# Three transposes for two per 128 slots, and both scatters of a one-unit block behind its second pair of ReLUs

## The chip, the cores and the metric

The kernel runs on one core of one Trainium2 chip. The metric is the device time of one execution in microseconds (us). Before the change three runs took 1338.32, 1340.45 and 1340.85 us; the median is 1340.45 us.

## The reference

A convolution over 7 tokens is followed by a mixture of experts. `x` has 8 sequences of 3584 tokens with 192 channels. Each of 8 heads (24 channels) has 7 taps, made from `weight` by a softmax. The result of the convolution goes to 8 experts: each token uses one, the one with the largest gate logit, or the expert of the token before it where a local gate is at 0.5 or above.

```python
x = einsum('hk,bskhg->bshg', softmax(weight), windows(x))      # 8 x 3584 x 192
logits = x @ w_gate                                            # 192 x 8
local  = sigmoid(x @ w_local)
for b, s:
    e = argmax(logits[b, s]) if s == 0 or local[b, s] < 0.5 else e_before
    out[b, s] = softmax(logits[b, s])[e] * (relu(x[b, s] @ w1[e]) @ w2[e])   # 192 -> 1024 -> 192
```

All arithmetic is in 32-bit floats.

## The kernel before

**Tiles and stages.** The 28,672 tokens are cut into 16 parts of 1792. For each part the kernel computes the convolution (VectorE, line 388, with a first tap on ScalarE, line 378), the gate logits and the route, and then scatters every token's row from SBUF to its slot in a DRAM tensor `slots`, in which the slots of one expert lie together. A row (`DG` = 259 floats) holds a scale, a token number, the 192 channels from column `Y0` on, 64 channels once more (columns `Y0 + D` to `IX`), and the token number as an integer. A scatter is an indirect DMA of GpSimd (line 777, issued by `put`), 128 rows at a time.

**Blocks.** The expert layers run over blocks of slots. A unit is 128 slots of one expert; a block has one unit (n = 1) or two (n = 2). The trace has 142 blocks: first 35 of one unit, which run while the first parts are still being made, then 87 of two units, then 20 of one unit. A block needs its expert's weights (one tile `wb`, 1536 KB, line 906, loaded three blocks ahead into one of four buffers) and its rows (`xg`, line 913).

**One block in TensorE's order.** `hidden` multiplies the rows, channels on partitions (`xT`), by `w1` (line 963) in two halves of 24 matmul instructions in the trace each; after each half ScalarE writes two ReLUs into `hT` (line 968). Below they are called the first and the second pair of ReLUs. Then `turn` makes `xT` of the next block: it transposes `xg` on TensorE (line 360) into PSUM, `xps`, and ScalarE copies it to SBUF (lines 947 and 949). Then `output` multiplies `hT` by `w2` (line 980): the first half of its matmuls reads what the first pair of ReLUs wrote, the second half needs the second pair. ScalarE scales one half of the result (line 988), VectorE adds the other (line 992), and GpSimd scatters it to the output (line 996). All these orders are written out by hand; every engine runs its list in that order. `step` puts convolution and routing work in between, by times written in the code.

**Halves.** Each matmul works on 64 partitions, and two such matmuls, one for each half of the partitions, run beside each other. Of the 192 channels each half therefore sees three groups of 64 (`KD` = 3, index d), in an order that the host writes into `w1` (`_w1_layout`). `turn` before the change transposes two pieces of 128 columns per unit, each for both halves of the slots (`turn_half`): four transposes per unit. These give both halves of the partitions two of their three groups; the third one lies in PSUM on the other half of the partitions, and ScalarE copies it across (line 949, one copy for each half).

**Scatters of slots between ReLUs.** `hidden` calls `put(relu)` after each pair of ReLUs, for every block but the first: the scatter is made to wait for that ReLU. `shares=(1, 1)` says how many scatters go behind each pair. Nothing is issued when no rows are waiting. In blocks of two units a third may go behind the copy of `turn`.

Of the kernel before, what the change touches and what calls it, by code (L numbers as in the profile page):

```python
# [17 lines left out]
P = 128  # L18
# [63 lines left out]
def kernel(  # L82
# [112 lines left out]
    def wide(g, xv, y_sb, both):  # L195

        lps = yps_p.tile([P, 512], F32, name="yps")[:, :4 * TB].rearrange("p (q s) -> p q s", s=TB)  # L200
        count = [0]

        def mine():
            count[0] += 1
            return both and count[0] % 2 == 0

        def convolve(half, heads):
            bs = slice(half * NH, (half + 1) * NH)
            for h in heads:
                ps = hps_p.tile([P, 512], F32, name="hps")[:TB, :NH * GS]  # L210
                nc.tensor.matmul(ps, lhsT=hank[:NI, h, :],
                                 rhs=xv[:NI, bs, h * GS:(h + 1) * GS], start=True, stop=True)
                to = y_sb[:TB, bs, Y0 + h * GS:Y0 + (h + 1) * GS]
                at = ps.rearrange("p (b d) -> p b d", d=GS)
                if mine():
                    nc.vector.tensor_scalar(to, at, rz[:TB, h:h + 1], None, Alu.mult)
                else:
                    nc.scalar.activation(to, at, Act.Copy, scale=rz[:TB, h:h + 1])
                yield

        def again(half):
            bs = slice(half * NH, (half + 1) * NH)
            nc.gpsimd.tensor_copy(yr[:, bs, :], y_sb[:TB, bs, Y0 + P:Y0 + D])
            nc.gpsimd.tensor_copy(y_sb[:TB, bs, Y0 + D:IX], y_sb[:TB, bs, Y0 + P:Y0 + D])

        def turned(half, qs):
            at = half * 3 * NH // 2
            for q in qs:
                tps = hps_p.tile([P, 512], F32, name="hps")[:, :4 * TB].rearrange(
                    "p (u s) -> p u s", s=TB)  # L230
                for u in range(4):
                    b = half * NH + (q * 4 + u if q < 2 else 2 * u)
                    src = (y_sb[:TB, b, Y0:Y0 + P] if q < 2
                           else yr[:, b:b + 2, :].rearrange("p b d -> p (b d)"))
                    nc.tensor.transpose(tps[:, u, :], src, identity=ident[:TB, :TB])
                leave = nc.vector.tensor_copy if mine() else nc.scalar.copy
                leave(yT[:, at + 4 * q:at + 4 * q + 4, :], tps)
                yield

        def products():  # L240
            for j in range(4):
                u = j // 2 * 3 * NH // 2 + j % 2 * 4
                nc.tensor.matmul(lps[Q * j:Q * j + Q], lhsT=wgb[:, 0, :], rhs=yT[:, u:u + 4, :],
                                 start=True, stop=False, skip_group_check=True)
            for i in range(2):
                for j in range(4):
                    u = j // 2 * 3 * NH // 2 + NH + j % 2 * 2
                    nc.tensor.matmul(lps[Q * j:Q * j + Q, i::2, :], lhsT=wgb[:, 1 + i, :],
                                     rhs=yT[:, u:u + 2, :], start=False, stop=(i == 1),
                                     skip_group_check=True)  # L250

        yield from convolve(0, range(H))
        zy = z_tile()
        yT = zy[:, :3 * NH * TB].rearrange("p (u s) -> p u s", s=TB)
        yr = zy[:TB, 3 * NH * TB:].rearrange("p (b d) -> p b d", d=DR)
        again(0)
        yield from convolve(1, range(5))
        yield from turned(0, (0, 1))
        yield from convolve(1, range(5, H))
        yield from turned(0, (2,))  # L260
        again(1)
        yield from turned(1, range(3))
        products()
        if both:
            nc.vector.tensor_copy(lsb[:, :2, :], lps[:, :2, :])
            nc.scalar.copy(lsb[:, 2:, :], lps[:, 2:, :])
        else:
            nc.scalar.copy(lsb, lps)
        yield
        ltp = yps_p.tile([P, 512], F32, name="yps")[:TB].rearrange("p (q c) -> p q c", c=P)  # L270
        for q in range(4):
            nc.tensor.transpose(ltp[:, q, :], lsb[:, q, :], identity=ident)
        lt = sm.tile([P, NB, E + 1], F32, name="lt")[:TB]
        mark["lt", g] = nc.vector.tensor_copy(lt.rearrange("p (j q) e -> p j q e", q=4),
                              ltp.rearrange("p q (j c) -> p j q c", c=Q)[:, :, :, :E + 1])
        got[g] = lt
# [77 lines left out]
    def halves():  # L354
        return [(half, slice(half * DR, (half + 1) * DR)) for half in range(2)]
# [203 lines left out]
    def gathered(ps):  # L559
        xg = xp.tile([P, KT, DG], F32, name="xg")  # L560
        nc.scalar.copy(xg[:, 0, :Y0 + D], ps[:, :Y0 + D])
        nc.scalar.copy(xg[:, 0, Y0 + D:IX], ps[:, Y0 + P:Y0 + D])
        nc.scalar.copy(xg.bitcast(I32)[:, 0, IX:], ps[:, 1:2])
        return xg

    def logits(g, y_sb):

        nc.gpsimd.tensor_copy(y_sb[:, :, Y0 + D:IX], y_sb[:, :, Y0 + P:Y0 + D])  # L568
        z = z_tile()[:, :NT * D].rearrange("p (t d) -> p t d", d=D)
        for t in range(0, NT, TQ):  # L570
            u = min(t + TQ, NT)
            nc.vector.transpose(z[:, t:u, :], y_sb[:, t:u, Y0:Y0 + D])  # L572
            yield 0.2 * (u - t)
        yield "hop"


        lps = [hps_p.tile([P, TQ * Q], F32, name="hps") for half in range(2)]
        begin = [min(TQ * j, NT - TQ) for j in range(4)]
        for b in range(DQ):
            for j in range(4):  # L580
                for half, rows in halves():
                    nc.tensor.matmul(lps[half][Q * j:Q * j + Q, :], lhsT=wgq[rows, b, :],  # L582
                                     rhs=z[rows, begin[j]:begin[j] + TQ, b * Q:(b + 1) * Q],
                                     start=(b == 0), stop=(b == DQ - 1))
        ls = sm.tile([P, 2, TQ * Q], F32, name="ls", bufs=1)
        for half in range(2):
            nc.scalar.copy(ls[:, half, :], lps[half])
        yield "hop"
        lq = sm.tile([P, 2 * TQ, Q], F32, name="lq", bufs=1)
        nc.vector.transpose(lq.rearrange("p t e -> p (t e)"), ls.rearrange("p h x -> p (h x)"))  # L590
        yield 0.4
        lt = sm.tile([P, NT + 2, E + 1], F32, name="lt")
        for r in range(4):
            for j in range(4):
                t, u = TQ * j, min(TQ * (j + 1), NT)
                at = r // 2 * TQ + t - begin[j]
                e0 = r % 2 * (E + 1)
                nc.vector.tensor_copy(lt[Q * r:Q * r + Q, t:u, :],  # L598
                                      lq[Q * j:Q * j + Q, at:at + u - t, e0:e0 + E + 1])
                yield 0.12  # L600
        return lt
# [328 lines left out]
    def turn(n, xg):  # L930


        xps = xps_p.tile([P, 2, 512], F32, name="xps")
        at = xps[:, :, :BT].rearrange("p h (d k s) -> p h d k s", d=2, k=KT)
        for d in range(2):
            for k in range(n):
                src = xg[:, k, Y0 + d * P:Y0 + (d + 1) * P]
                for half in range(2):
                    turn_half(at[:, half, d, k, :], src, half)
        xT = tp.tile([P, KD, BT], F32, name="xT")  # L940
        to = xT.rearrange("p d (k h s) -> p h d k s", k=KT, h=2)
        first, by = to[:, :, :2], at
        if n == KT:
            first, by = [a.rearrange("p h d k s -> p h (d k) s") for a in (first, by)]
        else:
            first, by, to, at = [a[:, :, :, 0, :] for a in (first, by, to, at)]
        nc.scalar.copy(first, by)  # L947
        for half, rows in halves():
            copied = nc.scalar.copy(to[rows, :, 2], at[(DR, 0)[half]:(P, DR)[half], :, 0])  # L949
        return xT, copied  # L950

    def hidden(n, wb, xT, shares=(1, 1)):
# [4 lines left out]
        for two in range(2):  # L957
# [8 lines left out]
            for half in range(2):  # L966
                m = half * 4 + two * 2
                relu = nc.scalar.activation(hT[:, m:m + 2, w], hps[half][:, :, w], Act.Relu)  # L968
            for _ in range(shares[two]):
                put(relu)  # L970
        return hT

# [195 lines left out]
def _w1_layout(np, w1):  # L1168


    w = w1.reshape(E, KD, DR, 2, F // 2).transpose(0, 3, 2, 1, 4)
    w = np.stack([w[:, 0][:, :, [0, 2, 1]], w[:, 1][:, :, [1, 2, 0]]], 1)
    return w.reshape(E, P, KD * F // 2)


# [57 lines left out]
```

## Time and profile before

| what | value |
|---|---|
| median of three runs | 1340.45 us |
| the profiled execution's own time | 1340.85 us |
| its span, first to last instruction | 1339.1 us |
| TensorE busy (line 360: transposes) | 1315.2 us (60.3 us) |
| ScalarE busy (lines 947 and 949: copies of `turn`) | 583.9 us (72.2 and 92.4 us) |
| GpSimd busy (line 777: scatters to `slots`) | 492.8 us (228.0 us) |
| VectorE busy | 778.6 us |

The profiled execution's own time is 0.4 us above the median, and 1.75 us of it lie outside the span. Busy time of TensorE is the union of its matmuls, whose ends are modelled, so 98% busy is not 98% of its peak; the distance from the start of one block to that of the next tells more. A row of the timeline gives start, length, engine, line, operation, tiles, shapes and count, and in brackets how long the engine was idle before it and what ended that. One matmul in the code is two in the trace; one transpose is one.

### The profile page before, as it was taken

What the parts mean: (1) busy time and instruction counts of PE and PEld (TensorE: products, weight loads), DVE (VectorE), ACT (ScalarE), POOL (GpSimd) and SP (SyncE); (2) the same over time, 40 slices, a digit from 0 to 9 for tenths busy, and PEclk for the clock granted to TensorE, in tenths of its full rate; (3) what the DMA queues carried; (4) which work ended last, traced back from release to release, by engine and by line L of the source; (5) the groups of instructions that cost most, each with busy time, mean ns of one, the idle gap of its engine ahead of it and who ended that gap; (6) DMA issues with size and microseconds to landing.
All of it is one profiled execution on the core that took longest, in us unless ns stands there. A gap on an engine that the chain in (4) does not pass through costs nothing. (4 is left out here: it accounts for less than half of the span.)

```text
span 1339.1 us, 41274 instructions
## 1 busy us (share of the span) xinstructions
PE 1315.2 (98%) x16682; PEld 1264.3 (94%) x16682; DVE 778.6 (58%) x2434; ACT 583.9 (44%) x1431; POOL 492.8 (37%) x538
## 2 busy tenths in 40 slices
PE   8899999999999999999999999999999999999997
PEld 7898999899999999999999999999999999999997
DVE  5878887877777777868786878786520000000000
ACT  5244544444444444444444444444334333334443
POOL 4455443534343434343434343434344211121111
PEclk9899999999999999999999999999999999999999
DMA  4799999977575857675767675756566655556893
GB/s 180 262 357 406 376 352 356 365 281 276 192 287 189 295 197 286 209 274 208 274 209 274 208 281 207 288 204 234 206 234 230 207 185 184 190 192 235 322 332 124
DMA packets 67298, 340.36 MB, mean 254 GB/s; under 512 B 12576, under 2 KB 23191, under 8 KB 47650
## 3 DMA queue, kind: packets, MB, share of 16 engines
q1 hardware_dynamic: 44784, 284.88, 59.2%
q0 software_dynamic: 22320, 52.82, 10.4%
q8 instruction: 133, 2.18, 0.6%
q14 instruction: 59, 0.48, 0.1%
q10 hardware_dynamic: 2, 0.00, 0.0%
HBM read 284.73 MB, written 53.41 MB: 253 GB/s over the span
## 5 line engine op out<-in xcount | busy, mean ns | idle before, releaser
L980 PE MATMUL yps<-wb,hT 64*128 64x192 f32 x7328 | 647.0, 326 | 8.2 <-ACT hT L968 5.3
L963 PE MATMUL hps<-xT,wb 64*128 64x256 f32 (+1 forms) x6816 | 634.5, 336 | 1.6 <-issue 1.2
L980 PEld LDWEIGHTS yps<-wb,hT 64*128 64x128 f32 x7328 | 603.7, 187 | 19.6 <-ACT hT L968 10.8
L963 PEld LDWEIGHTS hps<-xT,wb 64*128 64x128 f32 x6816 | 585.1, 187 | 28.7 <-issue 3.2
L996 POOL DMA_INDIRECT out_dram<-o_sb,xg x229 | 232.4, 1015 | 608.6 <-DVE o_sb L992 540.1
L968 ACT ACTIVATE hT<-hps 128x512 f32<-128x512 f32 (+1 forms) x568 | 262.1, 512 | 393.1 <-PE hps L963 271.6
L388 DVE SCALAR_TENSOR_TENSOR y_sb<-x_sb,c,y_sb 128x336 f32<-128x336 f32 x672 | 376.1, 569 | 20.1 <-ACT y_sb L378 2.0
L992 DVE SCALAR_TENSOR_TENSOR o_sb<-yps,xg,o_sb 128x192 f32<-128x192 f32 x229 | 87.5, 413 | 475.7 <-ACT o_sb L988 468.5
L777 POOL DMA_INDIRECT slots<-y_sb,posi x228 | 228.0, 1000 | 207.4 <-ACT hT L968 81.6
L988 ACT ACTIVATE o_sb<-yps,xg 128x192 f32<-128x192 f32 x229 | 86.9, 418 | 305.4 <-PE yps L980 299.7
L949 ACT COPY xT<-xps 64x256 f32<-64x256 f32 (+1 forms) x284 | 92.4, 325 | 7.0
L947 ACT COPY xT<-xps 128x512 f32<-128x512 f32 (+1 forms) x142 | 72.2, 509 | 5.9 <-PE xps L360 2.9
L360 PEld LDWEIGHTS xps<-ident,xg 64*128 64x128 f32 x916 | 60.2, 139 | 5.2
L378 ACT ACTIVATE y_sb<-x_sb,c 128x336 f32<-128x336 f32 x112 | 63.7, 581 | 1.0
L360 PE MATMUL xps<-ident,xg 64*128 64x64 f32 x916 | 60.3, 221 | 0.0
L572 DVE STREAM_TRANSPOSE z<-y_sb 128x768 f32<-128x768 f32 (+1 forms) x56 | 45.4, 852 | 0.4
L598 DVE COPY lt<-lq 32x36 f32<-32x36 f32 x224 | 41.0, 183 | 3.5
L582 PE MATMUL hps<-z,wg 64*32 64x128 f32 x1344 | 24.1, 272 | 0.7 <-issue 0.5
L582 PEld LDWEIGHTS hps<-z,wg 64*32 64x32 f32 x1344 | 19.0, 105 | 3.1 <-issue 2.3
L556 PE MATMUL yps<-y_sb 112*128 112x194 f32 x64 | 13.8, 377 | 1.8 <-DVE y_sb L550 1.8
L556 PEld LDWEIGHTS yps<-y_sb 112*128 112x128 f32 x64 | 12.5, 220 | 2.6 <-DVE y_sb L550 2.0
L568 POOL COPY y_sb<-y_sb 128x896 f32<-128x896 f32 x14 | 13.4, 954 | 0.0
(240 smaller groups left out, 384.0 us busy)
## 6 DMA issues: line engine op xcount, KB each, us to landing
wb<-in_w_dram SPq DMA_DIRECT2D x138, 1536.0 KB
x_sb<-in_x_dram SPq DMA_DIRECT2D x14, 1920.0 KB
xg<-slots SPq DMA_DIRECT2D x87, 259.0 KB
xg<-slots SPq DMA_DIRECT2D x53, 129.5 KB
wb<-in_w_dram SPq DMA_DIRECT2D x12, 512.0 KB
out_dram<-o_sb,xg POOLq DMA_INDIRECT x229
slots<-y_sb,posi POOLq DMA_INDIRECT x228
x_sb<-in_xb_dram SPq DMA_DIRECT2D x4, 768.0 KB
```

The costliest lines, as they stand in the source:

```text
L360: nc.tensor.transpose(to, src[rows], identity=ident[rows, rows])
L378: nc.scalar.activation(cols(h), chans(h, 0), Act.Copy, scale=c[:, h, 0:1])
L388: nc.vector.scalar_tensor_tensor(cols(h), chans(h, k), c[:, h, k:k + 1], cols(h), Alu.mult, Alu.add)
L777: ins = nc.gpsimd.indirect_dma_start(out=slots[:, :], in_=rows, in_offset=None, out_offset=bass.IndirectOffsetOnAxis(ap=to, axis=0)).ins
L947: nc.scalar.copy(first, by)
L949: copied = nc.scalar.copy(to[rows, :, 2], at[(DR, 0)[half]:(P, DR)[half], :, 0])
L963: nc.tensor.matmul(hps[half][:, j, w], lhsT=wb[rows, f0:f0 + P], rhs=xT[rows, d, w], start=(d == 0 and j == 0), stop=(d == KD - 1), skip_g ...
L968: relu = nc.scalar.activation(hT[:, m:m + 2, w], hps[half][:, :, w], Act.Relu)
L980: nc.tensor.matmul(yps[half][:, k * D:(k + 1) * D], lhsT=hT[rows, m, k * P:(k + 1) * P], rhs=wb[rows, WA + m * D:WA + (m + 1) * D], start= ...
L988: nc.scalar.activation(o_sb[:, k, :], y[k][0], Act.Copy, scale=xg[:, k, 0:1])
L992: nc.vector.scalar_tensor_tensor(o_sb[:, k, :], y[k][1], xg[:, k, 0:1], o_sb[:, k, :], Alu.mult, Alu.add)
L996: sent = nc.gpsimd.indirect_dma_start(out=out, in_=o_sb[:, k, :], in_offset=None, out_offset=bass.IndirectOffsetOnAxis(ap=xg.bitcast(I32)[ ...
```

## The change

Two things are changed at once.

- `turn` transposes three pieces of 128 columns per unit in place of two, so that all three groups of 64 channels arrive on both halves of the partitions, and ScalarE copies all of them with one instruction; the two copies across partitions are gone. Columns `Y0 + D` to `IX` of a row now repeat the first 64 channels in place of the last 64 (three lines), and the host's order of `w1` follows.
- In blocks of one unit both scatters wait for the last ReLU of the second pair; before, one waited for the first pair and one for the second. Blocks of two units are as before.

```diff
     # again(), gathered() and logits(): what a row repeats
-            nc.gpsimd.tensor_copy(y_sb[:TB, bs, Y0 + D:IX], y_sb[:TB, bs, Y0 + P:Y0 + D])
+            nc.gpsimd.tensor_copy(y_sb[:TB, bs, Y0 + D:IX], y_sb[:TB, bs, Y0:Y0 + DR])
...
-        at = xps[:, :, :BT].rearrange("p h (d k s) -> p h d k s", d=2, k=KT)
-        for d in range(2):
+        at = xps[:, :, :KD * BT // 2].rearrange("p h (d k s) -> p h d k s", d=KD, k=KT)
+        for d in range(KD):
             for k in range(n):
-                src = xg[:, k, Y0 + d * P:Y0 + (d + 1) * P]
+                src = xg[:, k, Y0 + d * DR:Y0 + (d + 2) * DR]
                 for half in range(2):
                     turn_half(at[:, half, d, k, :], src, half)
...
-        first, by = to[:, :, :2], at
         if n == KT:
-            first, by = [a.rearrange("p h d k s -> p h (d k) s") for a in (first, by)]
+            to, at = [a.rearrange("p h d k s -> p h (d k) s") for a in (to, at)]
         else:
-            first, by, to, at = [a[:, :, :, 0, :] for a in (first, by, to, at)]
-        nc.scalar.copy(first, by)
-        for half, rows in halves():
-            copied = nc.scalar.copy(to[rows, :, 2], at[(DR, 0)[half]:(P, DR)[half], :, 0])
+            to, at = [a[:, :, :, 0, :] for a in (to, at)]
+        copied = nc.scalar.copy(to, at)
...
-            for _ in range(shares[two]):
+            for _ in range(shares[two] if n == KT else (0, sum(shares))[two]):
                 put(relu)
...
-    w = np.stack([w[:, 0][:, :, [0, 2, 1]], w[:, 1][:, :, [1, 2, 0]]], 1)
+    w = np.stack([w[:, 0], w[:, 1][:, :, [1, 2, 0]]], 1)
```

The engines' lists change only there: TensorE gets six transposes for four per unit, ScalarE one copy for three per block, and GpSimd, VectorE and the load queue keep theirs in the same order.

More of the change, by code (lines that the diff above doesn't have):

```diff
@@ L561, in gathered @@
         nc.scalar.copy(xg[:, 0, :Y0 + D], ps[:, :Y0 + D])
-        nc.scalar.copy(xg[:, 0, Y0 + D:IX], ps[:, Y0 + P:Y0 + D])
+        nc.scalar.copy(xg[:, 0, Y0 + D:IX], ps[:, Y0:Y0 + DR])
         nc.scalar.copy(xg.bitcast(I32)[:, 0, IX:], ps[:, 1:2])
@@ L566, in logits @@
     def logits(g, y_sb):
-        nc.gpsimd.tensor_copy(y_sb[:, :, Y0 + D:IX], y_sb[:, :, Y0 + P:Y0 + D])
+        nc.gpsimd.tensor_copy(y_sb[:, :, Y0 + D:IX], y_sb[:, :, Y0:Y0 + DR])
         z = z_tile()[:, :NT * D].rearrange("p (t d) -> p t d", d=D)
```

## The prediction

> **What bounds the kernel now.** I read the page first, for the share of each engine. TensorE is busy nearly all the time and the transposes are a small group of its work.
>
> ```profile
> span 1339.1 us, 41274 instructions
> PE 1315.2 (98%) x16682; PEld 1264.3 (94%) x16682; DVE 778.6 (58%) x2434; ACT 583.9 (44%) x1431; POOL 492.8 (37%) x538
> ...
> L360 PE MATMUL xps<-ident,xg 64*128 64x64 f32 x916 | 60.3, 221 | 0.0
> ```
>
> So time added to TensorE's list is paid, unless TensorE was waiting at that place. The waits view, second, says who waits for whom (total, times, longest); its row for the ReLUs is odd, since no ReLU reads a transpose.
>
> ```profile
> ACT hT L968 <- PE xps L360: 100.2, 61, 2.2
> ```
>
> Third, the timeline of TensorE around the last two-unit blocks: a block with eight transposes, one with four, and the start of the next.
>
> ```profile
> 1201.60 5.34 PE L963 MATMUL hps<-xT,wb 64*128 64x256 f32 x48
> 1206.78 0.41 PE L360 MATMUL xps<-ident,xg 64*128 64x64 f32 x8
> 1207.03 5.42 PE L980 MATMUL yps<-wb,hT 64*128 64x192 f32 x64
> 1212.28 5.34 PE L963 MATMUL hps<-xT,wb 64*128 64x256 f32 x48
> 1217.46 0.28 PE L360 MATMUL xps<-ident,xg 64*128 64x64 f32 x4
> 1217.58 5.42 PE L980 MATMUL yps<-wb,hT 64*128 64x192 f32 x64
> 1222.84 2.84 PE L963 MATMUL hps<-xT,wb 64*128 64x128 f32 x48
> ```
>
> The first block lasts 1212.28 - 1201.60 = 10.68 us, the second 10.56; they differ in four transposes, so four transposes are 0.12 us, 30 ns each, on the path.
>
> Fourth, the timeline of an early one-unit block with scatters:
>
> ```profile
> 196.67 2.84 PE L963 MATMUL hps<-xT,wb 64*128 64x128 f32 x48
> ...
> 199.38 0.97 POOL L777 DMA_INDIRECT slots<-y_sb,posi  x1 [0.30 <-issue]
> ...
> 199.47 1.52 PE L980 MATMUL yps<-wb,hT 64*128 64x192 f32 x16
> ...
> 200.85 0.66 ACT L968 ACTIVATE hT<-hps 128x256 f32<-128x256 f32 x2 [1.93 <-PE xps L360]
> 201.29 1.57 PE L980 MATMUL yps<-wb,hT 64*128 64x192 f32 x16 [0.30 <-ACT hT L968]
> ...
> 201.78 0.96 POOL L777 DMA_INDIRECT slots<-y_sb,posi  x1 [1.43 <-ACT xT L947]
> ...
> 202.69 2.85 PE L963 MATMUL hps<-xT,wb 64*128 64x128 f32 x48
> ```
>
> and of a late one, where no scatter to the slots is left:
>
> ```profile
> 1266.96 2.85 PE L963 MATMUL hps<-xT,wb 64*128 64x128 f32 x48
> ...
> 1269.83 0.66 ACT L968 ACTIVATE hT<-hps 128x256 f32<-128x256 f32 x2 [0.62 <-PE hps L963]
> ...
> 1272.41 0.84 PE L963 MATMUL hps<-xT,wb 64*128 64x128 f32 x12
> ```
>
> The late block lasts 5.45 us and its second pair of ReLUs starts at 2.87. The early one lasts 6.02 and the pair starts at 4.18, although its matmuls ended at 196.67 + 2.84 = 199.51, and the pair waits for nothing but TensorE's semaphore. It starts 0.50 us after the scatter at 199.38 ends. I read this as: TensorE's signals arrive late while a scatter is issued, up to some 1.45 us after its start. TensorE then stands at 201.29 for the second pair. Seventeen one-unit blocks show this pattern, most 6.00 to 6.06 us long. In two-unit blocks the same scatter costs nothing: 703.46 to 714.14, with scatters, is also 10.68, since there the first half of line 980 (2.6 us) covers the late pair.
>
> **The change part by part.**
>
> *Transposes.* TensorE gets two more per unit. The 87 two-unit turns get four each: 87 x 0.12 = 10.4 us, beside no wait, so all on the path. The 55 one-unit turns get two each: 55 x 0.06 = 3.3 us. Where TensorE waited for the late ReLUs this would be hidden; I count it whole because that wait goes with the second edit. Together 13.7 us. Bounds: the page's busy time per transpose, 60.3 / 916 = 66 ns, gives 458 x 0.066 = 30 us, but that interval also covers the neighbours' work; the least spacing of the starts, 27 ns, gives 12.4. I take 30 ns, which is a difference of whole blocks; below zero nothing can go, since no work is taken from TensorE.
>
> [...]
>
> *ScalarE's copies.* Removed are 592 + 2 x 367 ns per two-unit turn and 377 + 2 x 260 ns per one-unit turn. The new copy has 768 or 384 elements per partition; from 377 ns at 256 and 592 at 512 I extend to 807 and 485. ScalarE wins 0.5 or 0.4 us per block, about 87 x 0.519 + 55 x 0.412 = 68 us busy. On the path it is worth nothing: line 963 waited for `xT` for under 1 us in all, and ScalarE idles 393 us before its ReLUs. The cover is line 980, which runs beside the copy for 2.6 us or more. The copies in rows (lines 224, 562, 568) keep their size and read columns that are ready earlier: nothing.
>
> *Scatters.* GpSimd's list keeps its order; the first scatter of a one-unit block only starts later. Behind it wait the second scatter, the output scatter (line 996), the copy of line 568, and in the load queue the row loads that need a group's last scatter. Those, like the weights, are issued about three blocks ahead (a load at 196.90 for the block at 217.53), so a shift of 1.2 us is covered. Gain: the second pair no longer meets a scatter, 6.03 - 5.45 = 0.58 us in 17 blocks, 9.9 us at most from this pattern. Then the two scatters go back to back, from about 3.8 us into the block, and the second (about 5.05) meets TensorE's last signal of the block at 5.5. This pattern is in the trace too, where GpSimd ran late:
>
> ```profile
> 76.78 0.95 POOL L777 DMA_INDIRECT slots<-y_sb,posi  x1 [0.30 <-issue]
> ...
> 78.04 0.94 POOL L777 DMA_INDIRECT slots<-y_sb,posi  x1 [0.30 <-issue]
> 78.50 0.95 PE L963 MATMUL hps<-xT,wb 64*128 64x128 f32 x10
> 79.66 2.40 PE L963 MATMUL hps<-xT,wb 64*128 64x128 f32 x38 [0.21 <-issue]
> ```
>
> The pair straddles the end of a block; TensorE starts the next one at 78.50 and then begins nothing from 79.18 to 79.66. Such holes of 0.45 to 0.51 us follow the pairs at 71.26, 76.78, 82.37 and 103.54. Less a normal spacing of 0.055 that is 0.43 us per block, against 0.58 now. The gain is bounded by 0.58 and by the whole block: 78.50 to 84.58 is 6.08, 0.05 worse than now. I take 0.58 - 0.43 = 0.15 us, which is the direct row: 17 x 0.15 = 2.5 us.
>
> *Sum.* 13.7 - 2.5 = +11.2 us. The profiled execution's own 1340.85 becomes 1352.05; it lies 0.4 above the median, so 1351.6. This case alone spans 1348 to 1356.
>
> **Rivals.**
>
> *The hold vanishes.* If the signal held at the end of a block meets enough queued work on TensorE, all 9.9 us come back: 13.7 - 9.9 = +3.8, 1344.3. For it: pairs at 3.70 and 4.96 into the block at 98.58 left that block at 5.45. Against it: the next one took 6.86.
>
> *The hold becomes a ring.* Late signal, late line 988, late output scatter (about 1.15 after it), which then holds the second pair (1.4), then two scatters (1.35 and 1.25) and the hold of the last signal (1.75): 6.9 us per block if each waits for the one before, 0.87 more than now, 17 x 0.87 = 14.8, total +28.5, 1369. Half of it gives 1361.
>
> *Faster.* The one-unit blocks from 60.72 to 272.36 are 26.3 us longer than 5.45 each; four groups of gate matmuls (line 582; 1.59 us at 270.83) are 6.4 of that. If spaced scatters cause all the other 19.9, and a pair causes none, the change gives 13.7 - 19.9 = -6.2, 1334.2. It decides once more than 13.7 of the 19.9 go. Against it: these blocks run with DMA at 0.96 of its time and 369 GB/s (windows view, 60 to 275), and the best slice of the page has 406.
>
> *The transposes are hidden.* Then only the 2.5 us remain: about 1338, within 0.2%. It would need holes at line 360; its idle time is 0.0.
>
> **How the numbers follow.** Chances: forecast 0.52, hold vanishes 0.20, ring (in part or whole) 0.15, faster 0.07, hidden 0.06. The range 1343 to 1361 holds the first two and half a ring; beyond it lie the faster and hidden cases and the full ring. A measurement of this kernel tells 0.2%, about 2.7 us, from no change. Faster by more than that: 0.07. Within it: 0.09, the hidden case and 0.03 of the vanishing hold, which ends only 1.2 us above that bound. Slower: 0.84.
>
> **What would show it.** Right: 1374 transposes, two-unit blocks at 10.80, late one-unit blocks at 5.51, early ones near 5.9 with second pairs at about 2.9 to 3.9, scatters about 1.25 apart, and holes in line 963 after them. ScalarE's busy time falls by some 68 us without effect. Wrong: two-unit blocks at 10.68 (transposes free) or above 10.9; early blocks at 5.5 (hold vanished) or above 6.3 (ring).

## The result, and the profile after

The changed kernel takes 1353.26 us (median of four runs, 1352.75 to 1355.32), the kernel before 1339.84 us in the same comparison. The ratio is 1.0104, 95% interval 1.0087 to 1.0122: slower by 13.9 us (11.7 to 16.3). Forecast were 1351.6 us and a loss of 11.2.

The page of the changed kernel: span, busy times, and two groups of TensorE (busy time and mean ns of one, then idle time before them).

```profile
span 1351.8 us, 41874 instructions
PE 1327.2 (98%) x17140; PEld 1300.6 (96%) x17140; DVE 777.6 (58%) x2434; ACT 511.0 (38%) x1147; POOL 492.7 (36%) x538
...
L360 PE MATMUL xps<-ident,xg 64*128 64x64 f32 x1374 | 82.0, 222 | 0.2 <-issue 0.2
...
L582 PE MATMUL hps<-z,wg 64*32 64x128 f32 x1344 | 30.6, 273 | 4.4 <-issue 4.2
```

TensorE's busy time grew by 12.0 us, nearly the whole loss, and ScalarE's fell by 72.9 without effect. The last row is the one to stop at. The gate matmuls (line 582, the products that give the gate logits) were not changed, yet they take longer than on the page of before:

```profile
L582 PE MATMUL hps<-z,wg 64*32 64x128 f32 x1344 | 24.1, 272 | 0.7 <-issue 0.5
```

In the waits view the row of the late second pair has shrunk from 100.2 us to this:

```profile
ACT hT L965 <- PE xps L360: 17.6, 18, 1.9
```

So the hold of the early one-unit blocks, the wait for a late second pair of ReLUs, is mostly gone. The timeline of one of them (block 22) shows its new order:

```profile
187.10 2.85 PE L960 MATMUL hps<-xT,wb 64*128 64x128 f32 x48
...
188.97 1.06 POOL L993 DMA_INDIRECT out_dram<-o_sb,xg  x1 [0.80 <-DVE o_sb L989]
...
190.32 0.66 ACT L965 ACTIVATE hT<-hps 128x256 f32<-128x256 f32 x2 [0.92 <-PE xps L360]
...
191.26 1.05 POOL L777 DMA_INDIRECT slots<-y_sb,posi  x1 [1.22 <-ACT hT L965]
192.61 0.96 POOL L777 DMA_INDIRECT slots<-y_sb,posi  x1 [0.30 <-issue]
192.61 2.85 PE L960 MATMUL hps<-xT,wb 64*128 64x128 f32 x48
```

The second pair of ReLUs starts 3.22 us into the block (190.32 - 187.10), no longer at 4.18; the scatters follow at 4.16 and 5.51; and the next block begins after 5.51 us, the length of an undisturbed block, with no hole in its line 960.

The distances from block to block, added up by stage, tell where the loss lies (us; the other profiles are explained below):

| stage | before | after | transposes alone | release alone | after, gates kept clear |
|---|---|---|---|---|---|
| up to block 2 | 66.5 | 63.0 | 65.8 | 65.6 | 64.4 |
| 29 early one-unit blocks without gate matmuls | 173.7 | 166.5 | 174.2 | 165.7 | 165.3 |
| 4 early blocks with them | 32.1 | 37.7 | 31.5 | 39.8 | 34.4 |
| 77 two-unit blocks without | 823.8 | 833.7 | 833.3 | 823.8 | 833.1 |
| 10 two-unit blocks with | 126.7 | 133.2 | 133.1 | 128.6 | 125.0 |
| 20 late one-unit blocks | 116.3 | 117.7 | 117.5 | 116.5 | 117.8 |

From before to after: 77 plain blocks +9.9, late blocks +1.4, as the transposes should; 29 early blocks -7.2, far better than forecast; and the 14 blocks with gate matmuls +5.6 and +6.5, which the forecast did not have. The start varies from 63.0 to 66.5 us between profiles, without regard to the kernel: a second profile of before has 65.7, a second one of after 65.0. The -3.5 of this pair is not part of the change.

The timeline of a two-unit block with gate matmuls (block 83) before the change:

```profile
807.00 1.59 PE L582 MATMUL hps<-z,wg 64*32 64x128 f32 x96
...
808.39 1.11 POOL L777 DMA_INDIRECT slots<-y_sb,posi  x1 [1.79 <-DMA wb<-in_w_dram]
...
808.52 5.47 PE L980 MATMUL yps<-wb,hT 64*128 64x192 f32 x64
```

and in the changed kernel:

```profile
811.13 1.58 PE L582 MATMUL hps<-z,wg 64*32 64x128 f32 x94
...
812.32 1.11 POOL L777 DMA_INDIRECT slots<-y_sb,posi  x1 [1.78 <-DMA wb<-in_w_dram]
...
812.89 0.38 PE L582 MATMUL hps<-z,wg 64*32 64x128 f32 x2 [0.19 <-issue]
...
813.19 5.74 PE L977 MATMUL yps<-wb,hT 64*128 64x192 f32 x63
```

The scatter starts 7.02 us into the block in both. The gate matmuls start at 5.82 in place of 5.64, so now it comes 0.1 us before they would be through: two of 96 are left, and they start only at 812.89. The block lasts 13.33 us, where 10.80 and a gate of 1.59 make 12.4.

What TensorE loses there can be counted. In this profile the steps from the start of one gate instruction (weight load or matmul) to that of the next take 34 ns on average where they begin within 1.25 us of the start of one of GpSimd's indirect DMAs (457 steps, 15.7 us), and 7 ns elsewhere (2217 steps, 15.6 us). The average hides two kinds of steps: 19 stops of 0.40 to 0.59 us make 9.4 of the 15.7 us, and the other 438 steps take 14 ns each; elsewhere no step lasts 0.2 us. In each of the ten two-unit blocks with gate matmuls it is one stop of 0.42 to 0.50 us, which begins 0.06 to 0.14 us after the scatter's start. The wide matmuls of lines 960 and 977 need 28 to 54 ns for each instruction anyway (2.68 us for 96 in block 22, 5.18 us for 96 in a two-unit block), and a single scatter beside them mostly costs nothing: in 42 plain two-unit blocks of this profile one starts 6.9 to 7.15 us into the block, over line 977, no step of that line in the 1.4 us after the start is longer than 0.15 us, and 39 of the 42 blocks last 10.80 to 10.82 us. Why the gate matmuls stop there and these don't was not shown.

### The profile page after: what moved, and what is told of

It is laid out like the page before. It is cut to its first block, busy times and chain, and to the rows that moved or that the text cites. A ratio compares the mean times of both kernels' runs of the same rounds, so it can differ in the third digit from the quotient of the medians.

```text
span 1351.8 us, 41874 instructions
## 1 busy us (share of the span) xinstructions
PE 1327.2 (98%) x17140; PEld 1300.6 (96%) x17140; DVE 777.6 (58%) x2434; ACT 511.0 (38%) x1147; POOL 492.7 (36%) x538
## 5 line engine op out<-in xcount | busy, mean ns | idle before, releaser
L960 PE MATMUL hps<-xT,wb 64*128 64x256 f32 (+1 forms) x6816 | 641.2, 336 | 2.0 <-issue 1.8
L960 PEld LDWEIGHTS hps<-xT,wb 64*128 64x128 f32 x6816 | 612.4, 187 | 7.9 <-issue 4.3
L946 ACT COPY xT<-xps 128x768 f32<-128x768 f32 (+1 forms) x142 | 96.9, 682 | 3.0 <-PE xps L360 2.9
L360 PEld LDWEIGHTS xps<-ident,xg 64*128 64x128 f32 x1374 | 82.7, 139 | 2.8 <-issue 0.3
L360 PE MATMUL xps<-ident,xg 64*128 64x64 f32 x1374 | 82.0, 222 | 0.2 <-issue 0.2
L582 PE MATMUL hps<-z,wg 64*32 64x128 f32 x1344 | 30.6, 273 | 4.4 <-issue 4.2
L582 PEld LDWEIGHTS hps<-z,wg 64*32 64x32 f32 x1344 | 21.0, 105 | 11.6 <-issue 10.6
L590 DVE STREAM_TRANSPOSE lq<-ls 128x256 f32<-128x256 f32 x14 | 6.2, 443 | 15.4 <-ACT ls L587 15.4
L587 ACT COPY ls<-hps 128x128 f32<-128x128 f32 x28 | 6.1, 269 | 23.0 <-PE hps L582 20.2
```

Source lines behind the costliest of these rows:

```text
L360: nc.tensor.transpose(to, src[rows], identity=ident[rows, rows])
L946: copied = nc.scalar.copy(to, at)
L960: nc.tensor.matmul(hps[half][:, j, w], lhsT=wb[rows, f0:f0 + P], rhs=xT[rows, d, w], start=(d == 0 and j == 0), stop=(d == KD - 1), skip_g ...
```

## The experiments

Kernels under one heading ran on one chip; the headings are different chips. Differences in us are worked out from the ratio to the kernel before on the same chip (median 1338 to 1339 us).

### The two edits apart, and the gate blocks kept clear

*Transposes alone* (the changed kernel with the old release):

```diff
-            for _ in range(shares[two] if n == KT else (0, sum(shares))[two]):
+            for _ in range(shares[two]):
```

> The three transposes alone; scatters are released as before the change. Theory (gate): in the 14 blocks with gate matmuls (line 582) the last gate matmuls carry a semaphore update; eight to twelve transposes put them later by 0.12 to 0.18 us, into the scatter behind the second pair of ReLUs, and TensorE then stands still until that scatter's issue is over. Two-unit blocks: 87 x 0.12 plus 6 us in the ten with a gate, so 35 to 121 last 966.5 to 967.5 us against 950.5. In the early one-unit blocks the transposes lie in the hold behind the ReLUs: 6.03 us as before, so nothing in 17 blocks. In all +18 to +20 us, about 1358. The prediction's own sum for this part is +13.7 (1353.5). Rival (supply): the stall comes from too many short instructions in a row on TensorE; the time here is the same, the next kernels tell the two apart.

Measured: 1354.82 us, ratio 1.0116 (1.0096 to 1.0136), +15.5 us, less than the 18 to 20 expected (the profile is of an execution 2.3 us above the median). The two-unit stage lasts 966.5 us, as expected; ten gate blocks 133.1. Early blocks with the hold mostly stay at 5.98 to 6.04: there the transposes are free, since TensorE waits for the ReLUs anyway.

*Release alone* (the kernel before, with the other line of that diff):

> The release of both scatters by the second pair in one-unit blocks alone; two transposes as before. Theory (vanish): the hold of 0.58 us goes in 17 one-unit blocks and does not come back at the block's end, 9.9 us; four early blocks with gate matmuls give back 5 and two more blocks 2, so -3 us, about 1337; early blocks without a gate at 5.45, blocks 5, 15 and 34 at 9 to 10 us. Two-unit blocks unchanged at 950.5 in all. The prediction's theory (hold moves to the block's end): early blocks near 5.9, gate blocks as before, -2.5 us, 1337.3. The sums agree by chance; the blocks tell them apart.

Measured: 1336.75 us, ratio 0.9984 (0.9974 to 0.9993), -2.1 us. The 29 early blocks fall from 173.7 to 165.7 us, 19 of them to 5.45 to 5.51, and the four with gate matmuls rise from 32.1 to 39.8. The hold vanishes and does not move to the block's end; the gate blocks take nearly all of it back in this profile. (It is of an execution 4.9 us above the median; its block 25 has 12.00 us where before and after have 8.8.)

*After, with the gates kept clear*:

```diff
-            nc.scalar.copy(ls[:, half, :], lps[half])
+            st["ls"] = nc.scalar.copy(ls[:, half, :], lps[half])
...
+    LATEG = {5, 15, 34}
+    GATES = {25} | set(range(41, 96, 6))
...
-        hT = hidden(n, wbs[i], xT, (1, 1) if i else (0, 0))
+        shares, owed = (0, 0), 0
+        if i:
+            shares = (0, 2) if n == 1 and i not in LATEG else (1, 1)
+        if i in GATES:
+            first = 1 if n == KT else 0
+            owed = min(2 - first, max(len(to_put) - first, 0))
+            shares = (first, 0)
+        hT = hidden(n, wbs[i], xT, shares)
...
         step(2.1 if n == 1 else 4.2)
+        puts_behind(st.get("ls"), owed)
```

> The changed kernel, but in the 14 blocks with gate matmuls the scatters are kept away from them: in block 25 and the ten two-unit blocks the scatters behind the second pair wait for the copies of the gate sums (line 587); in blocks 5, 15 and 34 one scatter goes behind each pair, as before the change. Every engine's order is the changed kernel's. Theory (gate): the ten two-unit gate blocks fall from 13.3 to about 12.45 us (10.80 + 1.59), blocks 5, 15 and 34 from 10.27, 9.17 and 9.40 to about 8.2, 7.6 and 7.7, and the time from 1353.3 to 1339 (1337 to 1343). Rival (supply of short instructions): the two-unit gate blocks stay at 13.3 and only the early ones can move: 1347 to 1353.

Measured: 1341.54 us, ratio 1.0025 (1.0015 to 1.0035). Of the 13.9 us of loss 10.6 are gone by moving 14 blocks' scatters, with every engine's order unchanged. Block 83 now:

```profile
801.69 1.59 PE L582 MATMUL hps<-z,wg 64*32 64x128 f32 x96
...
803.22 5.47 PE L977 MATMUL yps<-wb,hT 64*128 64x192 f32 x64
...
804.07 0.96 POOL L777 DMA_INDIRECT slots<-y_sb,posi  x1 [2.78 <-ACT ls L587]
```

All 96 run through in 1.59 us and the scatter comes later; the ten blocks have 12.47 to 12.65 us. This chip is one where the two meet without the edit: the transposes alone gave 133.1 us in the ten blocks on it, the changed kernel 133.2 in the first comparison. Twelve transposes and 96 gate matmuls still stand in a row, so the number of short instructions alone is not the cause. Blocks 15 and 34 came to 8.18 (expected 7.6 and 7.7), and block 5 stayed at 9.79 (expected 8.2): its scatters, held up by GpSimd's copy of line 568 (0.98 us), and an output scatter right behind them still lie over its gate matmuls.

*Release alone, with the gates kept clear* (the same edit on two transposes):

> Two transposes, both scatters behind the second pair in one-unit blocks, and the gate blocks' scatters kept away as in the kernel before this one. Theory (gate): the two-unit gate blocks fall from 12.3 to 13.1 us to about 12.3 (4 us in all), blocks 5, 15, 34 stay as before the change, the hold is gone from 17 blocks: 1339.8 - 9.9 - 4 + 1 = 1327 (1324 to 1331), faster than both kernels. Rival (supply): no more than the release alone gives, 1337, or 1332 if the early blocks give back nothing.

Measured: 1332.52 us, ratio 0.9951 (0.9935 to 0.9967): faster than both kernels by 6.6 and some 20 us, but 1.5 above the range expected. The two-unit gate blocks have 124.9 us; the four early ones still 35.3, where about 32 were expected.

### Are the copies free; does the order of the scatters matter; what is a clear gate worth before

*Transposes repeated, copies kept* (the kernel before, and):

```diff
+        for k in range(n):
+            for half in range(2):
+                turn_half(xps[:, half, BT + k * DR:BT + (k + 1) * DR], xg[:, k, Y0:Y0 + P], half)
```

> The kernel before, with the first group of channels turned a second time into unused PSUM: as many transposes as the changed kernel has (1374), and all three copies of ScalarE per turn kept; the repeated transposes are read by nobody. Theory (copies are free): plain two-unit blocks at 10.80 us as in the changed kernel, so that the 73 us that ScalarE saves there are worth nothing on the path, and the gate blocks rise as they do there, to about 13.3; time as with the three transposes alone, 1354 (1351 to 1358). Rival (the saved copies were worth something that hides part of the transposes' price): blocks above 10.85, time above 1359.

Measured: 1351.39 us, ratio 1.0098 (1.0082 to 1.0115). Plain blocks last 10.80 or 10.81 with all the copies in place, so the copies that the change saves are worth nothing there. But eight of the ten gate blocks are at 12.48 to 12.60, not at 13.3: a miss, which the next heading explains.

*Both scatters behind the first pair*:

```diff
-            for _ in range(shares[two]):
+            for _ in range(shares[two] if n == KT else (sum(shares), 0)[two]):
```

> The kernel before, but in blocks of one unit both scatters wait for the first pair of ReLUs: output scatter, slot scatter, slot scatter in a row. Theory (TensorE's signals land about 1.45 us after a scatter's start, and three scatters in a row starve TensorE): the second pair of ReLUs, due at 2.87 us, starts at 4.2 where a signal gets through between the two scatters, and at 5.2 to 5.6 where none does; early one-unit blocks without a gate then last 6.0 or 7.1 to 7.5 us; a hole of 0.5 us in TensorE's list comes some 3.7 us after the first of three scatters. Time 1340 (all get through) to 1364 (17 x 1.3 more). Rival (the order of the scatters does not matter, the hold comes from something else of the first pair): blocks at 6.03, time within 0.3% of before.

Measured: 1348.58 us, ratio 1.0076 (1.0056 to 1.0096). The early blocks last mostly 6.4 to 7.2 us and the second pair starts at 4.4 to 5.2, between the two values expected. So the place of the scatters sets the length of the hold, and the rival falls; my rule for when a signal lands was too coarse. The hole behind three scatters appears in four blocks only; in the others TensorE stood waiting for the ReLUs at that time.

*The kernel before, gates kept clear* in block 25 and the two-unit blocks:

> The kernel before, with one edit: in block 25 and in the ten two-unit blocks with gate matmuls the scatters behind the second pair wait for the copies of the gate sums. Theory (TensorE takes short instructions slowly while a scatter is issued): the ten two-unit gate blocks go from 126.7 us in all to 124.0 (10 x 12.3 to 12.4), the hold in the early one-unit blocks stays; 2 to 3 us faster than before, ratio 0.998. Rival (nothing in the kernel before stands against a scatter there, its gate matmuls ended just ahead of it): no difference.

Measured: ratio 0.9998 (0.9989 to 1.0008); the ten gate blocks have 125.5 us. The time is the rival's: on this chip a scatter kept clear of the gates is worth nothing. The second profile of before, on another chip, has 125.6 us in these blocks without the edit (see below). The time before on this chip was the same as on the one above.

*No scatters in the early gate blocks*:

```diff
+    NONE = {5, 15, 25, 34}
+    GATES = set(range(40, 95, 6))
...
+        shares, owed = (0, 0), 0
+        if i and i not in NONE:
+            shares = (0, 2) if n == 1 else (1, 1)
+        if i in GATES:
+            owed, shares = min(1, max(len(to_put) - 1, 0)), (1, 0)
```

> Two transposes, both scatters behind the second pair in one-unit blocks, no scatter to the slots at all in the one-unit blocks with gate matmuls (5, 15, 25, 34; their scatters go one block later each), and in the two-unit gate blocks (now 40 to 94) the second scatter behind the copies of the gate sums. Theory (short instructions are slow during a scatter): the four early gate blocks fall from 35.3 us in all to 28 to 30 (5.45 + 1.59 each, and up to 0.5 for the output scatter that still meets them), so 1327 (1324 to 1330). Rival (it is the heavy DMA traffic there, not the scatters): they stay above 34 us, and the time at 1332 or above, since two scatters more then follow each other in later blocks.

Measured: 1335.68 us, ratio 0.9980 (0.9970 to 0.9989), worse than keeping them. The early gate blocks only fell to 32.6; that output scatters still meet the gates there is the author's reading. And the edit did more than it was meant to: the scatters put off changed the order of VectorE's and GpSimd's lists too. Block 37 lasts 15.66 us in place of 10.68: line 980 first waits 3.03 us for VectorE's line 992, which stands behind eight steps of the convolution, and then takes 6.98 us with two output scatters and three scatters to the slots beside it. So this kernel does not tell what the gates alone are worth.

### How far the gate blocks are the same in another execution

> The changed kernel once more, to see how far its gate blocks are the same in another execution. Theory (in the two-unit gate blocks the last gate matmuls and the second scatter meet within 0.1 us): their total is between 126 us (none meets) and 134 us (all meet), not always 133.2, while plain two-unit blocks stay at 10.80. Rival (the stall belongs to twelve transposes and 96 gate matmuls in a row, whenever the scatter comes): 133 us again.

Measured: 1350.02 us (two runs), ratio 1.0085 (1.0065 to 1.0105), so a loss of 11.4 us on this chip. Plain blocks are at 10.80 again; the ten gate blocks have 126.7 us in all, seven of them 12.47 to 12.51. Block 83 of this profile:

```profile
809.24 1.59 PE L582 MATMUL hps<-z,wg 64*32 64x128 f32 x96
...
810.69 1.05 POOL L777 DMA_INDIRECT slots<-y_sb,posi  x1 [1.85 <-DMA wb<-in_w_dram]
810.76 5.47 PE L977 MATMUL yps<-wb,hT 64*128 64x192 f32 x64
```

The scatter comes 7.09 us into the block; in the first profile of after it came at 7.02, and there it caught the last two matmuls. The shift is systematic. In two-unit blocks with a scatter at about 4.2 us the second pair of ReLUs starts 5.64 to 5.66 us into the block (median) in the first profiles of before and after and in the four kernels of the first heading; it starts at 5.74 to 5.75 in those of the second and third heading, whatever the kernel. In seven of the ten blocks that decides which of the two comes first, the end of the gate or the scatter, and with it some 5 of the 6.5 us in the table. Each chip was measured on one occasion, so chip and occasion can't be told apart, and why the pair starts 0.1 us later is open.

> The kernel before once more. The first block starts at 46 to 48 us as in all other profiles, not at 50.96; plain blocks at 10.68 and 5.45; the two-unit gate blocks between 123 and 128 us in all; the 17 held blocks at 6.0 to 6.1.

Measured: 1338.16 us; first block at 46.42 us, 125.6 us in the ten gate blocks, plain blocks at 10.68, the held blocks mostly at 6.06 to 6.11. Block 71 lasts 13.91 here, and 13.4 to 13.8 with its scatter kept clear in three kernels, after a break without a wait in line 980 (1.27 us here, 0.74 to 1.12 in those three); that one is not explained.

*The fastest version*: two transposes, gates kept clear, and the pair of scatters released by the first of the two ReLUs:

```diff
                 relu = nc.scalar.activation(hT[:, m:m + 2, w], hps[half][:, :, w], Act.Relu)
+                if half == 0:
+                    early = relu
...
-                put(relu)
+                put(early if n == 1 else relu)
```

> The kernel with two transposes, both scatters behind the second pair and the gate blocks' scatters kept away (1332.5 us), with one edit more: in one-unit blocks the two scatters wait for the first ReLU of the second pair in place of the second one, 0.28 us earlier. Theory (what is left there are stretches in which output scatter and two slot scatters follow each other without a break; each costs a hole of 0.5 us in TensorE's list): an earlier pair leaves room ahead of the next output scatter; blocks 5, 9, 10, 20 and 30, now 6.5 to 9.9, lose 0.5 each or more, 1328 to 1331. Rival (those stretches start where rows become ready late, whatever releases the pair): no difference, 1331 to 1334.

Measured: 1330.99 us, ratio 0.9942 (0.9925 to 0.9960), the fastest of all, but its interval overlaps that of the kernel without this edit. Blocks 2 to 34 take 198.3 us against 201.2; blocks 5, 9, 10 and 30 are over 1 us shorter each, blocks 15, 11 and 31 longer by 1.8, 0.9 and 0.7. Whether the last edit helps stays open.

## Why the prediction was right, point by point

**The sum.** Forecast 13.7 - 2.5 = +11.2 us; measured +15.5 (12.8 to 18.2) for the transposes alone, -2.1 (-3.5 to -0.9) for the release alone, +13.9 together. The transposes' term agrees within that interval. The scatters' net is near the forecast by luck: inside it two misses cancel, early blocks that gained far more (7.2 us from before to after) and gate blocks that the forecast had not priced (5.6 us lost in the four early ones). So the time lies within the range, but not for the reason given.

**Transposes.** Right for what was costed: four are 0.12 us in plain two-unit blocks (10.68 to 10.80) and two are 0.06 in undisturbed one-unit blocks (5.45 to 5.51). The 77 plain blocks and 20 late ones paid 11.3 us. The length of a record is not the price here: it is 222 ns on average, but 68 of the 77 blocks are at 10.80 or 10.81, which is 30 ns for each transpose more. What the term lacked is the company of other work: the gate matmuls start up to 0.3 us later (0.18 in block 83), and a scatter stands there. The page of before had the group (L582, 14 blocks), and the prediction used it only to subtract it from a rival. In the first comparison the ten blocks lost 6.5 us, on another chip 1.1, which is no more than their own transposes; there the forecast for the two-unit stage (+10.4) meets the +10.8 between the second profiles.

**ScalarE's copies.** Right: 164.6 us of copies became 96.9, 67.7 less where 68 were forecast, and the repeated transposes with all copies kept gave the same blocks.

**Scatters.** The net was right by luck (-2.5 forecast, -2.1 measured), its working was wrong. The step that failed is "Less a normal spacing of 0.055 that is 0.43 us per block": a hole at the start of the next block, taken from pairs of scatters near 76.78 and 78.04. In that stretch an output scatter at 75.41 came right before the pair. It was three indirect DMAs without a break, and TensorE stopped 3.77 us after the first of them began. The holes in line 960 of the changed kernel's early blocks (0.28 to 0.61 us, most of them near 0.5) all lie 2.9 to 3.8 us after the start of such a row of three (in block 5 a row with a break of 0.47 us). In the ordinary block there is a break between the output scatter and the pair (1.22 us in block 22), and no hole. So the rival "the hold vanishes", given 0.20, is what happened to the plain early blocks: 20 of 29 at 5.51 or 5.52, where 7 were free of the hold before. By the prediction's own sign, early blocks at 5.5, this part was wrong. What took the gain back was neither hole nor ring but the four early gate blocks: with two scatters back to back and the output scatter behind them, blocks 5, 15 and 34 went from 8.17, 7.54 and 7.62 to 10.27, 9.17 and 9.40 us.

**The ring** stayed in part: blocks 3, 4, 9, 10, 20 and 30, where a scatter slips to the end of the block or into the next one, last 6.0 to 6.9 us; before it was 6.0 to 7.3. **Hidden transposes**: only in the blocks with the hold, and only as long as the hold is there (transposes alone, 29 early blocks: 174.2 against 173.7).

## What to carry to other kernels

Here the removed stall was worth what the next collision left of it: 7.2 us gained in 29 early blocks, 5.6 lost in the four early gate blocks. So after moving an indirect DMA, look at what TensorE does in the 1.5 us after its start, above all at groups of short matmuls (the stops in the gate matmuls begin 0.06 to 1.10 us after it) and at the instructions that others wait for (the second pair of ReLUs starts some 1.4 us after it). When a cost is read from a pattern, look at what else is in the pattern: the hole belonged to three scatters in a row, and the pair that was moved had a break ahead of it. And where two events stand within 0.1 us of each other, price both orders: the ten gate blocks of the changed kernel took 133.2 us in one profile and 126.7 in another.

## What was not expected of the hardware

- Within 1.25 us of the start of an indirect DMA of GpSimd, TensorE takes a gate instruction in 34 ns on average, elsewhere in 7 (first profile of after); most of it is 19 stops of 0.40 to 0.59 us. Wide matmuls show such stops mostly where three or more such DMAs follow each other (0.28 to 0.61 us in line 960 of the changed kernel's early blocks, 2.9 to 3.8 us after the first of the three starts). But blocks 41, 47 and 53 of before also have one of 0.39 to 0.43 us in line 980, right behind the gate matmuls and 0.86 to 0.89 us after the start of a single scatter.
- The profile shows no wait ahead of most stops: 4.2 of the 4.4 us that TensorE idles before gate matmuls go to "issue" (line 582 on the page of after). That its instructions come late there is the author's reading. What delays them was not tried, nor whether GpSimd's issuing or the transfer itself is the cause. The DMA packets of queue q8, "instruction" on the page, don't go with the stops: in the ten two-unit gate blocks the last one began anywhere from 0.02 to 9.7 us before TensorE went on.
- The second pair of ReLUs starts some 1.4 us after a scatter's start in six profiles (at 5.64 to 5.66 us in two-unit blocks) and 0.1 us later in the other seven (5.74 to 5.75), the same in every profile of a chip. That TensorE's signals land late is read from this. In this kernel that moves seven blocks by some 0.85 us each.
